# One core, three layers in a hand-written order: all 1277 steps re-ordered, and one drain of GpSimd

## The chip, the cores and the metric

One NeuronCore of a Trainium2 chip. The metric is device microseconds of one execution; the kernel before was run three times: 381.22, 381.32 and 378.41 us, median 381.22.

## The reference

Three layers one behind the other, in float32 (cut to the core):

```python
# 1. WKV attention: r, k, v are (2, 8, 768, 48)
for t in range(S):
    cur = einsum('bhd,bhe->bhde', u * k[:, :, t], v[:, :, t])
    y[:, :, t] = einsum('bhd,bhde->bhe', r[:, :, t], state + cur)
    state = w * state + einsum('bhd,bhe->bhde', k[:, :, t], v[:, :, t])
# 2. gated FFN: x is (2, 768, 384), d_ff 1024
h = maximum(x @ w_in, 0)
conv = depthwise_conv3(h, conv_w)          # along the sequence
x = (h * sigmoid(conv)) @ w_out
# 3. one expert of 8 per token; the expert before is kept while the local gate is 0.5 or more
logits = x @ w_gate;  local = sigmoid(x @ w_local)
e = argmax(logits[b, s]) if s == 0 or local[b, s] < 0.5 else prev_e
out[b, s] = softmax(logits[b, s])[e] * (maximum(x[b, s] @ w1[e], 0) @ w2[e])
```

## The kernel before, in words

Products are formed from float16 halves: each float32 operand is split into a high part (ScalarE) and the low rest (VectorE or GpSimd), and PE makes three passes: high by high, high by low, low by high.

The attention runs in 12 chunks of 128 tokens and both batches of heads: decay (A), bonus (B), state (Z) and scores (Y), fed by loads (L) and tables (T, C). The FFN works on blocks of 256 hidden rows (G) and output tiles (O, and apart as OL for the logits and OR for the rows). WI and WO load and split its weights. Routing (R, Q, S) finds expert, slot and probability of each token and scatters the rows to a table of slots in DRAM on GpSimd; FE and F count the tokens per expert and make the lists of rows. F's last DVE line is L867.

The experts work on 14 tiles: 0 to 3 are full tiles of early tokens, 4 to 9 are pairs of half tiles with two experts each, 10 to 13 full tiles of later tokens. A tile's tokens are fetched by I: GpSimd gathers rows from slots into yb (L977), SP transposes them in the DMA into xsT (L993). ER loads the early rows er by two DMAs of SP, and EX multiplies them into place (L952, L954, xe). Each tile goes twice through U and D, once for each half of d_ff. U is nine products per half tile (L1049, ph), the split of the relu (ACT L1029 and DVE L1031, hr) and a transposition of hr into hT: eight PE transposes (L1061, the copy is L1064), or for the pairs a DMA transpose on SP (L1056). D multiplies hT with W2 (L1073, py); in the first half ACT scales (L1080), in the second DVE adds (L1082) and GpSimd scatters the rows to the output (L871). The weights W1 and W2 come by SP (L961, L967), 768 KB each into one of three staging buffers, and are split by ACT (L497) and DVE (L154).

Each of these works is a generator, and the order of everything is one written list, SEQ: every token advances the generator of its name by one step (up to its next yield). The engines PE, ACT, DVE and SP issue in exactly the order in which SEQ emits their instructions; GpSimd's instructions are chained in that order too (pool_order), except DMAs among themselves. So a step that is moved carries all its instructions, on every engine, with it. At the end a branch (L1126, on the number of tiles that 14 didn't cover, with the value loaded at L1125) holds a fallback that isn't taken with these inputs; L1168 is the end of the program.

Of the splits of hr:

```python
def relu_split(hi, lo, ps):
    nc.scalar.activation(out=hi, in_=ps, func=AF.Relu)
    yield
    nc.vector.scalar_tensor_tensor(out=lo, in0=ps, scalar=0.0, in1=hi, op0=ALU.max, op1=ALU.subtract)
```

Of the kernel before, what the change touches and what calls it, by code (L numbers as in the profile page):

```python
# [54 lines left out]
G_0_0_1 A_3 A_3 WI_2 WO_0 Y_2 B_3 B_3 B_3 Y_3 Y_3 L_5 L_5 L_5 L_5 Z_3 G_0_0_1 WI_2 Y_3 G_0_0_1 G_0_0_1 A_5 A_4 A_4 A_4 Y_2 Y_2 WO_1 Z_4 B_3 WO_0 WO_0
WI_2 Y_2 L_6 L_6 G_0_0_1 Y_4 WO_2 G_0_0_1 G_0_0_1 WO_0 WO_0 A_5 A_5 A_5 B_4 B_4 WO_0 WO_0 G_0_0_1 G_0_0_2 G_0_0_2 Y_3 Y_3 L_6 L_6 A_6 G_0_0_2 WO_1
G_0_0_2 WO_1 G_0_0_2 G_0_0_2 A_6 L_9 B_4 Y_4 G_0_0_1 A_5 A_6 Y_4 G_0_0_0 WO_1 G_0_0_0 G_0_0_2 G_0_0_0 B_5 Y_3 G_0_0_2 G_0_0_2 Z_6 WO_2 A_6 A_6 A_5 A_5
Y_4 WO_1 WO_1 G_0_0_0 Y_3 Y_3 L_7 L_7 Y_3 WO_1 Y_5 B_4 L_7 L_7 A_7 WO_1 WO_1 B_5 A_7 A_6 Y_4 Z_6 G_0_0_2 G_0_0_0 A_6 A_6 G_0_1_1 G_0_0_0 WO_2 A_7 B_5
# [24 lines left out]
G_1_2_2 OR_1_0 G_1_2_2 G_1_2_2 R_1_2_2 OR_1_1 W1_7_0 R_1_2_2 R_1_2_2 G_1_2_2 G_1_2_2 G_1_2_2 R_1_2_2 R_1_2_2 Q_1_2_2 OR_1_2 Q_1_2_2 OR_1_2 S_2 S_2
G_1_2_0 Q_1_0_2 Q_1_0_2 S_7 S_7 G_1_2_0 S_5 S_5 W1_7_0 G_1_2_2 OR_1_2 OR_1_2 G_1_2_3 FE G_1_2_2 OR_1_0 OR_1_0 G_1_2_3 G_1_2_0 S_3 S_3 OR_1_2 OR_1_2
G_1_2_2 W1_2_0 G_1_2_2 G_1_2_2 G_1_2_2 FE OR_1_0 OR_1_0 OR_1_0 W1_0_0 S_6 S_6 OL_1_5 OL_1_5 OR_1_3 OR_1_3 OL_1_4 OL_1_4 OR_1_3 OL_1_5 OR_1_3 OR_1_3
Q_1_2_2 OL_1_4 W1_1_0 W1_0_0 OL_1_4 FE W1_1_0 OR_1_3 OL_1_4 OL_1_4 OL_1_5 OL_1_5 OL_1_5 OR_1_5 R_1_4_2 OR_1_5 W1_1_0 VE VE R_1_4_2 R_1_4_2 OR_1_4
OR_1_4 W1_4_0 W1_4_0 R_1_4_2 R_1_4_2 R_1_4_2 S_8 S_8 S_9 S_9 OR_1_5 OR_1_5 R_1_4_2 R_1_4_2 W1_4_0 R_1_4_2 IO BL_0 Q_1_4_2 F OR_1_5 OR_1_5 OR_1_4
Q_1_4_2 Q_1_4_2 W2_2_0 ER ER I_1 I_0 OR_1_4 I_2 I_3 S_11 S_11 OH OH OR_1_4 OR_1_4 S_10 S_10 W1_2_0 W1_2_0 I_1 I_0 I_2 I_3 W2_1_0 EX EX EX EX F EX EX
EX EX U_0_1 EX EX EX EX U_0_0 U_0_2 U_0_3 W2_3_0 F M M U_0_1 U_0_1 BL_1 BL_2 I_6 I_7 U_0_4 W2_2_0 U_0_0 U_0_0 U_0_5 U_0_1 EJ W2_2_0 U_0_2 U_0_2 U_0_1
U_0_0 I_8 I_9 I_10 I_11 I_12 I_13 U_0_3 U_0_3 W2_1_0 U_0_0 U_0_4 U_0_4 U_0_2 W2_1_0 U_0_4 U_0_2 W2_6_0 I_6 U_0_5 U_0_5 V V U_0_3 U_0_5 I_7 U_0_6 U_0_3  # L90
W2_3_0 I_8 U_0_7 U_0_6 U_0_6 W2_3_0 U_0_6 I_9 W2_4_0 U_0_8 U_0_7 U_0_7 W2_6_0 U_0_7 I_10 U_0_9 W2_6_0 U_0_8 U_0_8 U_0_8 I_11 I_12 W2_7_0 U_0_10 W2_4_0
U_0_9 U_0_9 W2_4_0 U_0_9 W2_5_0 I_13 U_0_11 U_0_10 U_0_10 U_0_10 U_0_10 W2_7_0 U_0_12 U_0_11 U_0_11 W2_7_0 U_0_11 W2_0_0 U_0_11 U_0_13 W2_5_0 ME ME ME
U_0_12 U_0_12 W2_5_0 U_0_12 U_0_13 U_0_13 U_0_12 W2_0_0 U_0_13 W2_0_0 U_0_13 D_0_4 W1_5_1 D_0_5 D_0_4 W1_4_1 D_0_3 D_0_3 W1_4_1 D_0_2 D_0_2 W1_5_1
D_0_5 D_0_10 D_0_10 W1_3_1 W1_3_1 D_0_1 W1_4_1 W1_5_1 D_0_12 D_0_6 D_0_6 W1_6_1 W1_7_1 W1_3_1 W1_6_1 W1_6_1 D_0_13 W1_7_1 W1_7_1 U_1_4 D_0_13 W1_0_1
# [1078 lines left out]
```

## Time and profile before

| | us |
|---|---|
| median of three runs | 381.22 |
| the profiled execution | 378.47 |
| its span | 376.6 |
| PE busy | 322.8 (86%) |
| DVE busy | 260.8 (69%) |
| ACT busy | 192.1 (51%) |
| GpSimd (POOL) busy | 186.3 (49%) |
| mean granted TensorE clock | 0.941 |

All times in the views are microseconds from the start of the span of the profiled execution. A row of a timeline has start, duration, engine, line, operation and tiles, and in brackets how long the engine was idle before it and what released it. In a table of windows the busy time and the number of instructions of PE, PEld, DVE, ACT and POOL, in this order, stand behind the length of the stretch, then the mean granted clock of TensorE (1.00 is the higher of its two levels, 0.50 the lower), the DMA engines' share and GB/s.

### The profile page before, as it was taken

Reading aid. Unit: us, or ns where it says so; the run is one execution under the profiler, and the core shown is the slowest. Engines: PE = TensorE matmul, PEld = TensorE weight load, DVE = VectorE, ACT = ScalarE, POOL = GpSimd, SP = SyncE. Lnnn points to the kernel's source line nnn. Section 1 sums busy time; section 2 is a strip of 40 time slices with the busy share of each in tenths; the row PEclk is TensorE's granted clock in tenths of the full one; section 3 lists DMA queues with packets and bytes.
Section 4 is the critical chain, followed back from the end, with each engine's and each line's share of the span. In section 5 each row is a group of like instructions: output and inputs, shape, how many; then the busy total and the mean of one; then the engine's idle time right before and its main releaser. Section 6 shows DMA issues by size and latency. Waiting matters only on the chain. (4 is left out here: it accounts for less than half of the span.)

```text
span 376.6 us, 7931 instructions
## 1 busy us (share of the span) xinstructions
PE 322.8 (86%) x2859; PEld 223.1 (59%) x2859; DVE 260.8 (69%) x497; ACT 192.1 (51%) x343; POOL 186.3 (49%) x222
## 2 busy tenths in 40 slices
...
GB/s 203 224 187 222 161 166 123 102 127 77 128 150 89 84 138 23 158 243 179 46 162 191 240 240 44 222 60 229 266 204 174 225 258 256 278 39 57 126 95 52
DMA packets 106880, 58.81 MB, mean 156 GB/s; under 512 B 87171, under 2 KB 96599, under 8 KB 106836
## 3 DMA queue, kind: packets, MB, share of 16 engines
...
q14 instruction: 18, 0.15, 0.2%
HBM read 41.57 MB, written 5.96 MB: 126 GB/s over the span
## 5 line engine op out<-in xcount | busy, mean ns | idle before, releaser
L871 POOL DMA_INDIRECT out_dram<-yb x14 | 13.8, 987 | 117.1 <-DVE yb L1082 114.4
L1049 PE MATMUL ph<-w1h,xsT 128*128 (+1 forms) x144 | 49.7, 412 | 15.1 <-DMA xsT<-yb 15.1
L1073 PE MATMUL py<-w2h,hT 128*64 (+2 forms) x320 | 56.9, 327 | 0.0
L599 PE MATMUL psh<-x1T,wi_h 128*128 128x258 f16 (+2 forms) x288 | 49.5, 273 | 1.4 <-ACT hp L604 1.4
L1049 PEld LDWEIGHTS <-xsT 128*128 128x128 f16 (+1 forms) x216 | 22.7, 109 | 42.4 <-DMA xsT<-yb 16.0
L1073 PEld LDWEIGHTS <-hT 128*64 128x64 f16 (+1 forms) x480 | 34.4, 105 | 21.3 <-issue 2.8
L1031 DVE SCALAR_TENSOR_TENSOR hr<-ph,hr 128x512 f16<-128x512 f32 x28 | 18.9, 685 | 33.1 <-ACT hr L1029 30.0
L599 PE MATMUL psh<-x1T,wi_l 128*128 128x258 f16 (+2 forms) x144 | 39.3, 273 | 0.0
L154 DVE SCALAR_TENSOR_TENSOR w1l<-ws,w1h 128x1536 f16<-128x1536 f32 x16 | 27.9, 1755 | 14.8 <-ACT w1h L497 14.7
L1073 PE MATMUL py<-w2l,hT 128*64 128x384 f16 (+2 forms) x160 | 37.2, 326 | 0.0
L646 PE MATMUL psx<-wo_h,g_l 128*128 128x384 f16 (+2 forms) x144 | 35.9, 278 | 1.2 <-POOL g_l L152 1.2
L646 PE MATMUL psx<-wo_l,g_h 128*128 128x384 f16 (+2 forms) x144 | 36.6, 278 | 0.0
L152 POOL TENSOR_TENSOR g_l<-cv,g_h 128x512 f16<-128x512 f32 (+2 forms) x31 | 31.7, 1034 | 9.5 <-ACT g_h L163 9.4
L646 PE MATMUL psx<-wo_h,g_h 128*128 128x384 f16 (+2 forms) x144 | 36.3, 279 | 0.0
L154 DVE SCALAR_TENSOR_TENSOR w2l<-ws,w2h 128x1536 f16<-128x1536 f32 x16 | 28.0, 1753 | 7.1 <-ACT w2h L497 7.0
L599 PEld LDWEIGHTS <-wi_h 128*128 128x128 f16 x288 | 27.3, 98 | 7.2 <-issue 1.8
L1029 ACT ACTIVATE hr<-ph 128x512 f16<-128x512 f32 x28 | 16.7, 600 | 28.6 <-PE ph L1049 25.3
L646 PEld LDWEIGHTS <-g_h 128*128 128x128 f16 x288 | 22.5, 98 | 11.9 <-issue 1.1
L1049 PE MATMUL ph<-w1l,xsT 128*128 (+1 forms) x72 | 29.5, 409 | 0.0
L604 ACT ACTIVATE hp<-psh 128x258 f32<-128x258 f32 (+2 forms) x47 | 17.9, 383 | 21.1 <-PE psh L599 19.1
L497 ACT ACTIVATE w2h<-ws 128x1536 f16<-128x1536 f32 x16 | 23.7, 1488 | 9.1 <-DMA ws<-in_moe_w_dram 8.2
L1064 ACT COPY hT<-pt 128x1024 f16<-128x1024 f16 x16 | 16.1, 1016 | 19.7 <-PE pt L1061 19.7
...
## 6 DMA issues: line engine op xcount, KB each, us to landing
...
```

Of the source, the lines that this page charges most:

```text
L152: eng.tensor_tensor(out=lo, in0=src, in1=hi, op=ALU.subtract)
L154: nc.vector.scalar_tensor_tensor(out=lo, in0=src, scalar=scale, in1=hi, op0=ALU.mult, op1=ALU.subtract)
L497: nc.scalar.activation(out=hi, in_=src, func=AF.Copy, scale=scale)
L599: nc.tensor.matmul(ps[:, 0:n], lhsT=x[:, kk, ft * P:(ft + 1) * P], rhs=x1T[b][:, y, t0:t0 + n], start=(i == 0), stop=(i == 3 * NK - 1))
L604: nc.scalar.activation(out=hp[:, a, o:o + n], in_=ps[:, 0:n], func=AF.Relu, scale=2.0 ** -8)
L646: nc.tensor.matmul(ps[:, c0:c1], lhsT=x[part][:, ft, o:o + P], rhs=y[:, ft, c0:c1], start=(n == 0), stop=(n == 3 * NF - 1))
L871: q = nc.gpsimd.indirect_dma_start(out=dst, out_offset=bass.IndirectOffsetOnAxis(ap=idx.bitcast(U32), axis=0), in_=src, in_offset=None, bo ...
L1029: nc.scalar.activation(out=hi, in_=ps, func=AF.Relu)
L1031: nc.vector.scalar_tensor_tensor(out=lo, in0=ps, scalar=0.0, in1=hi, op0=ALU.max, op1=ALU.subtract)
L1049: nc.tensor.matmul(ps[hs], lhsT=xs_, rhs=part(W[("w1h", "w1l")[y]], o + kk * HF, HF), start=(n == 0), stop=(n == 3 * NK - 1))
L1064: nc.scalar.copy(out=W["hT"][i], in_=pt)
L1073: nc.tensor.matmul(ps[hs], lhsT=hT[:, x * KF + ft, hs], rhs=part(W[("w2h", "w2l")[y]], o + ft * DM, DM), start=(n == 0), stop=(n == 3 * KF ...
```

## The change

The list SEQ is written anew: the same tokens, each as often as before, in another order, and one token DR more. Trailing tokens of a generator that has nothing left stand at random places and do nothing. DR is a new step that issues one drain on GpSimd; it stands behind the last gathers of the late tiles and ahead of the first output scatter. The four hr buffers were four tiles of a list (popped when a tile's split begins, appended when it has been transposed); they are now taken in turn from a pool's tag with four buffers. The configuration is unchanged. Behind the two insertions lines move by 4 or 5: L1031 is L1036, L1056 is L1061, L1073 is L1076, L1125 is L1129, L1126 is L1130 and L1168 is L1172.

```diff
 SEQ = """
-C C LD C WI_0 C C WO_0 C C C CV C H_1 H_1 C C H_0 H_0 LD LD T T WI_3 LD C LD C WI_0 ...
...
+C C C LD C C WI_0 CV T LD C T T T T WO_0 LD L_2 WI_0 WI_0 C LD WI_0 CV C C LD T LD ...
...
-        W["hr"] = [late.tile([P, 2 * HF], F16, name=f"hr{i}") for i in range(4)]
+        late.tile([P, 2 * HF], F16, name="hr", tag="hr", bufs=4)
...
+    def drain():
+        nc.gpsimd.drain()
+        yield
...
-        hr = W["hr"].pop(0)
+        hr = W["late"].tile([P, 2 * HF], F16, name="hr", tag="hr", bufs=4)
         yield from relu_split(hr[:, 0:HF], hr[:, HF:2 * HF], ps)
...
-            W["hr"].append(hr)
...
-        W["hr"].append(hr)
...
+        "DR": drain,
```

Three places of the new order, engine by engine. First SP, behind the load of the expert numbers (ej) and ahead of the late tiles: ws is a staging buffer for expert weights, xsT6 and so on are late tiles' transposed tokens, hT4 and so on transposed hidden rows. Before:

```order
L1125 TENSOR_LOAD ej_140
L1125 ISA x2
L1056 DMA_TRANSPOSE hT4_3342<-hr0_3334 128x8x128
L967 DMA ws_3478<-in_moe2_w2_dram 128x4x384
L993 DMA_TRANSPOSE xsT6_3354<-yb1_3332 128x6x64
L1056 DMA_TRANSPOSE hT5_3343<-hr1_3335 128x8x128
L993 DMA_TRANSPOSE xsT7_3355<-yb1_3332 128x6x64
L993 DMA_TRANSPOSE xsT8_3356<-yb1_3332 128x6x64
L1056 DMA_TRANSPOSE hT6_3344<-hr2_3336 128x8x128
L993 DMA_TRANSPOSE xsT9_3357<-yb1_3332 128x6x64
L967 DMA ws_3558<-in_moe2_w2_dram 128x4x384
```

And now:

```order
L1129 TENSOR_LOAD ej_140
L1129 ISA x2
L967 DMA ws_3409<-in_moe2_w2_dram 128x4x384
L993 DMA_TRANSPOSE xsT6_3332<-yb1_3313 128x6x64
L993 DMA_TRANSPOSE xsT11_3337<-yb2_3314 128x6x128
L993 DMA_TRANSPOSE xsT10_3336<-yb2_3314 128x6x128
L993 DMA_TRANSPOSE xsT7_3333<-yb1_3313 128x6x64
L993 DMA_TRANSPOSE xsT12_3338<-yb2_3314 128x6x128
L967 DMA ws_3510<-in_moe2_w2_dram 128x4x384
L993 DMA_TRANSPOSE xsT8_3334<-yb1_3313 128x6x64
L1061 DMA_TRANSPOSE hT5_3321<-hr_3477 128x8x128
```

The hT transposes, which stood between the xsT ones, now stand behind six of them, and the first one is that of tile 5 and not 4.

Next DVE, in the last routing group: from the end of FE (rows1) to the one-hot oc, which PE needs (L736, pso). lg are the logits, xr the routed rows, w1l the low part of expert weights. Before:

```order
L812 TENSOR_TENSOR rows1_143<-em1_2919,jp_129 128x4
L154 SCALAR_TENSOR_TENSOR xr_125<-psx_2953,xr_125 128x384
L651 TENSOR_SCALAR lg_126<-psx_2966 128x9
L651 TENSOR_SCALAR lg_126<-psx_2940 128x9
L714 TENSOR_REDUCE mxs_136<-lg_126 128x2
L716 TENSOR_TENSOR oh_3045<-lg_126,mxs_136 128x16
L718 TENSOR_TENSOR oh_3045<-oh_3045,iom_127 128x16
L720 TENSOR_REDUCE mn_3048<-oh_3045 128x2
L721 TENSOR_TENSOR oh_3045<-iom_127,mn_3048 128x16
L723 TENSOR_SCALAR fr_3051<-lg_126 128x2
L727 TENSOR_TENSOR oc_3053<-oh_3045,fr_3051 128x2x8
L728 TENSOR_SCALAR oc_3053<-fr_3051 128x2x8
L154 SCALAR_TENSOR_TENSOR w1l_2279<-ws_3010,w1h_2278 128x1536
```

And now:

```order
L812 TENSOR_TENSOR rows1_143<-em1_3005,jp_129 128x4
L714 TENSOR_REDUCE mxs_136<-lg_126 128x2
L716 TENSOR_TENSOR oh_3073<-lg_126,mxs_136 128x16
L718 TENSOR_TENSOR oh_3073<-oh_3073,iom_127 128x16
L720 TENSOR_REDUCE mn_3076<-oh_3073 128x2
L721 TENSOR_TENSOR oh_3073<-iom_127,mn_3076 128x16
L723 TENSOR_SCALAR fr_3079<-lg_126 128x2
L727 TENSOR_TENSOR oc_3081<-oh_3073,fr_3079 128x2x8
L728 TENSOR_SCALAR oc_3081<-fr_3079 128x2x8
L154 SCALAR_TENSOR_TENSOR w1l_2300<-ws_2898,w1h_2299 128x1536
L742 SCALAR_TENSOR_TENSOR seq_133<-ca_3093,seq_133,pso_3088 8x256
L154 SCALAR_TENSOR_TENSOR w1l_2300<-ws_2760,w1h_2299 128x1536
```

The split of xr and the two logits, which stood between rows1 and mxs, are gone from there (they stand earlier), and the scan follows after one w1l as before.

Last GpSimd, at the end of the program; yb1 and yb2 hold the results of the tiles, out_0_dram is the output. Before:

```order
L986 MEMSET yb2_3333 128x4
L977 DMA yb2_3333<-slots_139,rows_146 128x392
L871 DMA out_0_dram<-yb2_3333 1536x384
L1126 UNCONDITIONAL_BRANCH
L1126 ISA
L1126 UNCONDITIONAL_BRANCH
L1168 ISA
```

And now:

```order
L977 DMA yb2_3314<-slots_139,rows_146 128x392
L871 DMA out_0_dram<-yb2_3314 1536x384
L1130 UNCONDITIONAL_BRANCH
L1130 ISA
L1130 UNCONDITIONAL_BRANCH
L871 DMA out_0_dram<-yb1_3313 1536x384
L1172 UNCONDITIONAL_BRANCH
L1172 ISA
```

Of the 14 output scatters one has moved behind the branch; before, all 14 stand ahead of it (the scatters of yb2 shown first in both belong to the fallback). GpSimd's gathers of late tiles are in the order 6, 11, 10, 13, 7, 12, 8, 9, where they were in the order 6 to 13, and the iota and the first blanking stand some routing groups earlier. On PE the matmul of F's count (L819), which stood ahead of the products of EX, is behind the first of six; D_0_5, D_0_4 and the transposes of the last tiles are set between the late U, where all late U stood ahead of D_0_4. On SP the two loads of er, which stood behind a W2 load, stand behind the load W1_2_0 and ahead of that W2 load. On DVE the tables RQ and G and narrowings of the weights WI_0 and WO_0 stand ahead of rT and kT at the start.

## Rows read from the trace of the kernel before

**Rows 1.** The windows of the stages (busy us, instructions, clock, DMA).
```profile
40.00:200.00 160.00, 151.85 (x1553) 120.61 (x1551) 138.62 (x297) 95.37 (x212) 121.78 (x153) 1.00 0.59 127
200.00:220.00 20.00, 13.61 (x89) 7.51 (x90) 14.10 (x41) 6.08 (x9) 9.63 (x10) 0.91 0.92 197
220.00:240.00 20.00, 12.65 (x102) 7.18 (x99) 12.40 (x34) 11.62 (x14) 13.15 (x14) 0.91 0.51 147
240.00:260.00 20.00, 11.45 (x77) 6.58 (x78) 6.99 (x7) 5.11 (x6) 0.00 (x0) 0.76 0.71 174
260.00:280.00 20.00, 16.52 (x109) 8.16 (x108) 8.53 (x8) 10.73 (x12) 0.00 (x0) 0.82 0.92 230
280.00:365.00 85.00, 84.59 (x684) 48.00 (x678) 43.10 (x41) 43.89 (x51) 10.88 (x11) 1.00 0.57 171
```

**Rows 2.** The waits of PE: us in all, times, longest.
```profile
PE ph L1049 <- DMA xsT<-yb: 15.1, 4, 8.7
```

**Rows 3.** PE's timeline from 202 to 277 us, at its gaps.
```profile
202.49 0.59 PE L736 MATMUL pso<-id,oc 128*8 128x128 f16 x4 [4.93 <-DVE oc L728]
...
214.66 0.38 PE L952 MATMUL pse<-idk,er 128*128 128x128 f16 x4 [3.90 <-DMA er<-slots]
...
243.75 0.58 PE L1049 MATMUL ph<-w1h,xsT 128*64 x1 [8.73 <-DMA xsT<-yb]
...
258.18 0.59 PE L1049 MATMUL ph<-w1h,xsT 128*128 x1 [3.31 <-DMA xsT<-yb]
...
271.10 0.59 PE L1049 MATMUL ph<-w1h,xsT 128*128 x1 [1.55 <-DMA xsT<-yb]
...
276.40 0.35 PE L1073 MATMUL py<-w2h,hT 128*64 128x384 f16 x2
```

**Rows 4.** SP's timeline from 204 to 260 us.
```profile
204.01 1.27 SPq L929 DMA_DIRECT2D er<-slots  x2
...
236.31 1.25 SPq L1056 DMA_TRANSPOSE hT<-hr  x1
...
238.37 1.21 SPq L993 DMA_TRANSPOSE xsT<-yb  x1
...
257.25 2.65 SPq L993 DMA_TRANSPOSE xsT<-yb  x2
```

**Rows 5.** GpSimd's timeline from 199 to 228 us.
```profile
199.63 0.62 POOL L938 IOTA places<- 128x512 f32 x1
200.17 1.40 POOL L985 MEMSET yb<- 128x1536 int32 x1
...
226.44 0.99 POOL L977 DMA_INDIRECT yb<-slots,rows  x1 [2.78 <-issue]
```

**Rows 6.** The timelines of DVE and PE at the start.
```profile
12.20 0.69 DVE L148 TENSOR_TENSOR rT<-ptf,Q 128x512 f32<-128x512 f32 x1 [0.25 <-PE ptf L325]
...
41.11 0.38 PE L599 MATMUL psh<-x1T,wi_h 128*128 128x256 f16 x2
```

**Rows 7.** DVE in routing: line L723 (ns min/median/max, first and last start), timeline.
```profile
L723 DVE TENSOR_SCALAR fr<-lg x4: 160/162/2145, 139.8 to 199.5; 128x2 f32<-128x2 f32 x3, 128x6 f32<-128x6 f32 x1
...
201.82 1.75 DVE L154 SCALAR_TENSOR_TENSOR w1l<-ws,w1h 128x1536 f16<-128x1536 f32 x1
...
212.70 1.76 DVE L154 SCALAR_TENSOR_TENSOR w1l<-ws,w1h 128x1536 f16<-128x1536 f32 x1 [0.66 <-ACT w1h L497]
...
225.81 0.15 DVE L867 TENSOR_TENSOR ej<-cc 1x1 int32<-1x1 f32 x1
```

**Rows 8.** The end: timeline, and GpSimd's queue in lines L1126 and L1168.
```profile
365.31 1.67 DVE L1082 SCALAR_TENSOR_TENSOR yb<-py,yb 128x384 f32<-128x384 f32 x3 [6.06 <-PE py L1073]
...
368.78 0.98 POOL L871 DMA_INDIRECT out_dram<-yb  x1 [0.30 <-POOLq L1126]
...
L1126 POOLq INC_SWDGE_SEM  x1: 940/940/940, 371.6 to 371.6; - x1
...
L1168 POOLq DRAIN  x3: 40/107/3177, 372.6 to 376.3; - x3
```

More of the change, by code (lines that the diff above doesn't have):

```diff
@@ L55 @@
[L55 to L58, printed above, removed]
@@ L83 @@
[L83 to L86, printed above, removed]
@@ L87 @@
[L87 to L94, printed above, removed]
@@ L99 @@
-U_1_9 U_1_3 W2_1_1 D_1_5 D_1_6 D_1_6 D_1_13 U_1_12 D_1_13 U_1_8 U_1_8 U_1_8 U_1_3 D_1_1 D_1_6 D_1_1 D_1_0 D_1_0 D_1_0 D_1_1 U_1_2 D_1_2 U_1_3 U_1_9
-D_1_12 U_1_3 D_1_12 D_1_3 D_1_8 D_1_5 U_1_9 U_1_7 D_1_8 U_1_10 U_1_7 U_1_10 D_1_13 U_1_10 D_1_9 D_1_3 D_1_3 D_1_8 D_1_12 D_1_9 D_1_9 U_1_10 U_1_10
-D_1_11 D_1_10 D_1_2 D_1_2 D_1_7 D_1_10 D_1_10 D_1_11 D_1_11 D_1_7 D_1_7
+C C C LD C C WI_0 CV T LD C T T T T WO_0 LD L_2 WI_0 WI_0 C LD WI_0 CV C C LD T LD C WI_3 C H_2 L_2 H_1 LD LD WO_0 A_0 T L_2 T A_1 A_0 A_0 C A_0 A_0
@@ new lines @@
+G_0_0_2 Y_3 G_0_0_2 Y_3 G_0_0_1 L_6 G_0_0_2 G_0_0_0 Y_4 WO_1 L_5 L_6 G_0_0_1 WO_0 A_5 B_4 G_0_0_0 Z_3 G_0_0_2 L_7 A_5 Y_3 A_6 A_5 Y_2 G_0_0_2 Y_2 A_5
+A_6 G_0_0_0 WO_1 A_6 A_6 Y_4 WO_1 Y_3 G_0_0_2 WO_0 WO_1 Y_4 Z_4 G_0_0_1 A_5 G_0_0_2 B_4 Y_4 WO_0 A_5 Y_3 L_7 G_0_0_0 G_0_0_2 Z_4 A_5 G_0_0_0 WO_1
+G_0_0_2 L_7 WO_2 L_7 G_0_0_2 Y_5 A_6 WO_1 WO_1 G_0_0_0 G_0_0_0 B_5 Z_6 Y_3 A_7 Y_4 WO_2 B_5 Y_3 H_1 G_0_0_0 Y_5 G_0_0_0 G_0_0_2 WO_1 G_0_1_1 G_0_1_2
+G_0_1_1 G_0_1_2 WO_1 G_0_1_1 Z_6 A_7 A_6 Y_5 A_6 L_8 WO_1 G_0_1_2 Y_4 WO_2 G_0_1_1 G_0_1_2 A_7 G_0_1_1 G_0_1_1 G_0_1_1 G_0_0_0 WO_0 G_0_1_1 A_6
@@ new lines @@
+B_7 WO_3 Y_7 WO_3 G_0_1_3 Y_7 A_8 G_0_1_3 B_7 G_0_0_3 Y_6 A_8 O_0_2 Y_7 A_8 G_0_2_0 G_0_0_3 O_0_2 G_0_1_3 WO_3 WO_3 RC G_0_2_0 O_0_2 Y_6 L_11 G_0_2_0
+G_0_2_0 A_8 L_9 B_7 G_0_2_0 WO_2 G_0_2_1 Z_8 Y_7 G_0_2_0 Y_6 Z_7 G_0_1_3 L_9 G_0_2_0 B_8 Y_7 WO_3 A_9 WO_3 G_0_2_1 A_9 A_8 G_0_2_0 A_8 B_7 WO_3 A_8
+G_0_2_1 A_9 G_0_2_0 Y_8 O_0_1 Y_7 L_10 L_11 O_0_1 B_8 A_9 G_0_2_1 G_0_2_1 A_9 O_0_1 G_0_2_1 G_0_2_1 G_0_2_0 G_0_2_1 G_0_2_2 Z_7 L_10 Z_8 G_0_2_2
+G_0_2_0 G_0_2_1 Y_7 L_10 O_0_2 Y_8 O_0_2 O_0_0 G_0_2_0 O_0_0 Y_8 G_0_2_1 O_0_1 A_9 L_10 Y_7 O_0_1 G_0_2_3 Z_8 A_9 G_0_2_2 A_9 B_8 Y_8 B_9 O_0_0 H_2
@@ new lines @@
+A_10 A_9 B_8 G_0_2_1 Y_8 O_0_0 G_0_2_3 W1_6_0 G_0_2_2 Z_9 O_0_3 O_0_2 O_0_1 G_0_2_1 Y_9 G_0_2_2 G_0_2_2 Y_8 B_9 Y_9 Y_9 G_0_2_2 A_10 Y_7 Z_9 Y_8 O_0_2
+Y_6 G_0_2_2 G_0_2_3 A_10 G_0_2_2 G_0_2_2 O_0_3 A_10 Y_9 A_10 G_0_2_3 Y_8 G_0_2_2 Z_10 Y_8 G_0_2_3 G_0_2_3 G_0_2_3 G_0_2_2 O_0_1 RC O_0_4 O_0_4 L_11
+G_1_0_3 G_1_0_3 O_0_4 G_0_2_3 G_1_0_3 G_0_2_3 G_1_0_3 Z_8 SI G_1_0_3 G_1_0_3 A_10 Y_9 O_0_3 G_1_0_3 L_11 A_10 G_0_2_3 G_0_2_3 A_11 G_1_0_1 A_10
+G_0_2_3 O_0_3 A_10 Z_9 G_1_0_1 G_1_0_3 B_9 WO_3 B_10 Y_10 O_0_5 O_0_4 O_0_3 O_0_3 O_0_3 Y_10 A_11 B_10 H_0 W1_5_0 G_1_0_1 O_0_5 G_1_0_3 G_1_0_3
@@ new lines @@
+R_0_0_6 G_1_1_1 G_1_1_1 G_1_1_1 OL_1_1 G_1_1_1 G_1_1_2 R_0_0_6 G_1_0_2 G_1_1_1 G_1_1_1 G_1_0_2 G_1_1_3 BL_0 R_0_0_6 G_1_1_2 OL_1_1 G_1_1_2 G_1_1_1
+OL_1_1 G_1_1_2 R_0_0_6 G_1_1_2 G_1_1_2 G_1_1_1 OL_1_1 OL_1_1 G_1_1_3 Q_0_0_6 G_1_1_3 G_1_1_3 G_1_1_3 R_0_0_6 OL_1_0 OR_1_1 G_1_1_3 G_1_1_2 OR_1_1
+G_1_1_3 G_1_1_3 OL_1_0 OL_1_0 OL_1_0 G_1_1_1 G_1_1_0 W1_6_0 G_1_1_1 R_0_0_6 S_3 G_1_1_2 OL_1_0 G_1_1_3 OR_1_1 G_1_1_2 G_1_1_3 OL_1_1 G_1_1_2 G_1_1_0
+R_1_0_2 W1_5_0 G_1_2_1 G_1_2_1 G_1_1_0 G_1_1_2 W1_6_0 G_1_2_1 W1_3_0 G_1_1_0 G_1_2_1 G_1_2_1 X W1_5_0 G_1_1_0 G_1_1_2 S_4 G_1_2_1 W1_7_0 G_1_2_1
@@ new lines @@
+OR_1_2 Q_1_2_2 G_1_2_0 IO W1_0_0 G_1_2_2 R_1_2_2 OR_1_3 OR_1_2 G_1_2_0 OR_1_2 OR_1_2 W1_1_0 Q_1_2_2 OR_1_0 S_0 R_1_2_2 R_1_2_2 OR_1_3 G_1_2_2 W1_1_0
+G_1_2_2 R_1_2_2 R_1_2_2 FE Q_1_2_2 OR_1_0 G_1_2_2 S_4 OR_1_0 S_7 OR_1_3 G_1_2_2 OR_1_3 R_1_2_2 OL_1_4 S_2 W1_4_0 S_8 OR_1_0 OL_1_4 OL_1_5 OL_1_5
+OL_1_5 FE OR_1_3 OL_1_5 S_6 OR_1_3 S_9 OL_1_4 OL_1_3 OL_1_4 OL_1_5 OR_1_4 W1_2_0 OR_1_4 ER OL_1_4 OR_1_4 FE R_1_4_2 I_2 ER R_1_4_2 R_1_4_2 W1_1_0
+W1_2_0 R_1_4_2 S_8 W1_4_0 S_1 OR_1_5 OR_1_5 W2_2_0 R_1_4_2 R_1_4_2 OR_1_4 OR_1_4 OR_1_5 OR_1_4 R_1_4_2 I_2 R_1_4_2 Q_1_4_2 VE OR_1_5 R_1_4_2 OH I_3
@@ new lines @@
+Q_1_4_2 OR_1_5 W1_2_0 OH I_1 EX EX F I_1 EX Q_1_4_2 EX F OR_1_5 I_0 EX S_10 EX EX S_11 I_3 EX EX VE F EX EJ I_0 EX EX W2_6_0 U_0_2 U_0_0 M W2_2_0
+U_0_1 S_0 ME W2_2_0 BL_1 U_0_0 U_0_2 U_0_1 U_0_0 W2_3_0 V U_0_4 U_0_2 I_6 BL_2 W2_1_0 I_11 U_0_1 U_0_1 I_10 W2_1_0 I_13 S_7 U_0_0 V U_0_5 I_6 W2_1_0
+U_0_2 I_7 I_12 W2_6_0 U_0_5 I_8 U_0_3 U_0_4 I_11 I_10 U_0_0 I_7 U_0_5 U_0_11 S_5 I_12 W2_4_0 U_0_4 U_0_10 W2_6_0 U_0_11 U_0_11 U_0_3 I_8 U_0_11 U_0_3
+U_0_7 WO_1 U_0_3 U_0_5 W2_7_0 U_0_10 W2_3_0 I_13 W2_4_0 W2_4_0 U_0_6 M S_3 U_0_3 W2_5_0 U_0_11 U_0_7 W2_7_0 U_0_1 U_0_10 U_0_7 U_0_12 I_9 U_0_4 S_11
```

58 lines of the change are left out of this document (26 added, 32 removed).

## The prediction

> **What bounds the kernel now.** I read the windows first, then PE's waits, PE's gaps, and only then the other engines beside each gap. The windows [rows 1] show two stages that PE fills and one that it does not. From 40 to 200 us PE is busy 151.85 of 160 us, and from 280 to 365 us 84.59 of 85, both at full granted clock. Between 200 and 280 us it is busy 13.61 + 12.65 + 11.45 + 16.52 = 54.23 of 80 us, and the granted clock there is 0.91, 0.91, 0.76 and 0.82: part of even that busy time runs at the lower of the two levels. So 25.8 us of waiting lie in one stage, the turn from routing to the experts, and an order that only moves steps can win there and hardly anywhere else. The list of PE's waits [rows 2] names the largest reason: 15.1 us in four waits for xsT, the transposed tokens of the late tiles. The gaps [rows 3] place them: 4.93 us before 202.49 (routing's one-hot on DVE), 3.90 before 214.66 (the early rows er), 8.73 before 243.75, 3.31 before 258.18 and 1.55 before 271.10 (xsT, with a small fourth). PE is past the first half's U at 276.40, where D_0_4 starts.
>
> The SP rows [rows 4] say why xsT is late. The gathers on GpSimd begin at 226.44 [rows 5]. The first late transpose leaves SP only at 238.37, because the hT transpose of U_0_4 stands ahead of it and waits until 236.31 for its hr. The later ones are laced with five more hT transposes and with weight loads, so that SP issues xsT as late as 257.25. PE used the first 243.75 - 238.37 = 5.4 us after its issue.
>
> **The change part by part.** The sum is made against the profiled execution: 378.47 us, span 376.6 and 1.9 around it. The shown runs have their median at 381.22, 2.75 above it; one of the three (378.41) is as fast.
>
> Start. The tables RQ and G and two narrowings of weights move ahead of rT on DVE, which stands at 12.20 [rows 6]; rT then comes some 5 us later. The weight chain behind it ends at about the same place in DVE's order, and the first gate matmul, now at 41.11, needs both. Bounds: 5 us lost (nothing made up) to 3 won (rT's chain is not last, the weights are). I take -0.5, near the cover, since the same DVE work stands ahead of that matmul.
>
> Attention and gate stage. 151.85 of 160 us are PE work that the change neither adds to nor removes. At most 8.15 us can be won. On the other side nothing but DVE's own slack holds: DVE is busy 138.62 of 160. I take -1, range -4 to +8.
>
> Routing. DVE's chain to the one-hot stands at lg and mxs behind a copy of xr, and its L723 takes 2.15 us [rows 7], beside IOTA and MEMSET on GpSimd from 199.63 to 201.57 [rows 5]. The line's other instructions take 0.16. The new order puts the chain directly behind rows1, and IOTA and blanking far earlier. If both come true, R, the moment at which the one-hot is done (201.82), comes 0.6 + 2.0 us earlier; bounds 0 and 2.6; I take 1.8, so R = 200.0.
>
> The Trainium skill, page "SBUF — State Buffer", section "Who interferes with whom", says that DVE and GpSimd share one pair of ports and that whoever issues second is blocked for the other's whole instruction. By it the 2 us go wherever the two overlap, and may come back where the new order sets DVE's small steps beside another GpSimd memory operation; the row agrees with the blocking, no row shows the new places. By the rule alone R would gain 2.0 and not 1.8.
>
> Early rows. The two loads of er now stand behind the third weight load W1_2_0, whose buffer is freed by a split that DVE does two splits later: one split (the one at 201.82) is 1.75 us [rows 7], and two with the small steps between end at R + 3.9. Before, er was issued at 204.01 [rows 4] = R + 2.2, and PE could go on at 214.66 = R + 12.8. Issued at R + 4.6, the same transfer ends at R + 15.2. This is 2.4 us given back, and PE waits here about 9 us instead of 3.9. The count F#1, whose matmul stood ahead of EX, stands behind EX's first step now, so the numbering on DVE starts at R + 16.3. Before it was itself held by a split (212.70 to 214.45 [rows 7]) and ended at 225.96 = R + 24.1; that split stands behind it now, and it ends at R + 25.1 by the same 8 us of steps. The gathers follow 0.5 us later: R + 25.5 = 225.5, against 226.44: -0.9.
>
> Late tiles. No hT transpose stands ahead of the first six late xsT on SP now; each waits for its own gather alone. A GpSimd DMA is counted as landed 2.8 us after its start (368.78 to 371.6 [rows 8]); the transpose and its landing take the 5.4 us seen above, and the first late tile is the second in order, 1.3 us on. So the first full wait ends 2.8 + 1.3 + 5.4 = 9.5 us, with two hand-overs between queues some 10.1 us, after the first gather, where it took 243.75 - 226.44 = 17.3: -7.2. From the first late U to the last (U_0_13) went 271.10 - 243.75 = 27.4 us. In the new order the last one's transpose stands behind a W2 load that waits for a split behind U_0_7; counting splits of 1.75 and tiles of nine matmuls, it starts at R + 55.5 = 255.5, 20 us after the first (R + 35.6): -7.4. Behind the last one stood 276.40 + 4.0 (D_0_4 and D_0_5) - 271.10 = 9.3 us; now D_0_5, waiting for its weights until about R + 59, D_0_4, the transposes and U_0_9 end at R + 67.7, 12.2 us on: +2.9. Together -0.9 - 7.2 - 7.4 + 2.9 = -12.6. Against it stands the clock. After 8.73 us idle the windows show it at 0.76; the wait before EX is now of that length, and EX and the first U behind it, some 6 us, may run at the lower level. +2.6, range 0 to 5. I take -10 for the stage; range -16 (two thirds of the idle gone) to 0 (the time only changes its place).
>
> Second half. 84.59 us of PE work without a gap. The weights of the second half start loading about as far ahead of the first U_1 as before, but reach it with a reserve of some 5 us. What the earlier end takes away of this cover costs +1.5, range 0 to 5.
>
> The end. Three L1082 follow the last matmul at 365.31, the last scatter starts at 368.78, GpSimd counts its transfers until 372.5 and then drains for 3177 ns [rows 8]. Two things change. The added drain stands where GpSimd idles for 90 us, so that it costs nothing itself; if the last drain's time goes with the DMAs since the one before, 14 instead of 38 leave 1.2 of 3.2 us. And the last scatter now stands behind the branch, so it waits for the landing of all others and for the 0.94 us that follow. One of these two gives up to 2 and the other costs about 0.8: -1.2, range -3 to +2.
>
> Sum: -0.5 - 1 - 10 + 1.5 - 1.2 = -11.2, 378.47 - 11.2 = 367.3. Two of three runs lie above the profiled one, so I forecast 368.
>
> **The rivals.** (a) The slack only changes place. The wait before EX grows (9 against 3.9), F#1 stands behind it, and the gathers start 2 or 3 us later than before instead of 0.9 earlier, if R gains nothing and er lands late; the idle clock eats the rest. For it: the longest chain through here is not PE's but DVE's and the DMAs'. Against it: the hT transposes did stand ahead of xsT in SP's rows. Then the stage gives 5 instead of 10, the reserve of W1 is gone, and start and middle give nothing: 378.47 - 5 + 3 = 376.5, between 373 and 381.
> (b) Slower. In the stage from 40 to 200 us DVE is 87% busy and in strict order. A new order of all its steps that meets the waits of PE, ACT and GpSimd less well makes DVE the bound there. At 78%, 138.62 / 0.78 = 178 us stand in place of 160: 18 us more, less 10 in the turn: 378.47 + 18 - 10 = 386. It decides from about 14 us of lost overlap on. For it: rT 5 us late at the start of every chain. Against it: PE's 0 to 1.4 us idle per window says that a good interlacing exists, and the steps of one chain keep their order.
> (c) More than I count: all xsT waits go, the clock stays up, and the start and the end win too: 378.47 - 15.1 - 3 = 360.
>
> **How the numbers follow.** Forecast (363 to 373) 0.50, (c) 0.11, (a) 0.23, (b) 0.16. This kernel's measurements can tell about 1% from no change, so faster is below 377.4 and slower above 385.0. Forecast, (c) and a third of (a) are faster: 0.69. The rest of (a) is within 1%: 0.15. (b) is slower: 0.16. The range leaves out the half of (b) beyond 386 and the far end of (c): 358 to 386.
>
> **What would show it.** Right: PE's gaps before xsT are one of about 9 us before EX and two or three below 4 us; L723 takes 0.2; SP issues the first six late xsT without an hT between; D_0 starts near 262 to 268; the last scatter stands alone behind the others' landing, and the last drain is near 1.2 us. Wrong: PE's idle time between 40 and 200 us above 12 us (then (b)); the first late U not before 241 (then (a)); a drain of 3 us at the end again (then the added drain does nothing).

## The result, and the profile after

| | before | after |
|---|---|---|
| median | 380.29 us (4 runs, 378.41 to 381.32) | 358.48 us (4 runs, 356.92 to 359.28) |
| ratio, 95% interval | | 0.9427 (0.9373 to 0.9481) |
| the profiled execution, its span | 378.47, 376.6 | 358.66, 356.8 |
| PE busy | 322.8 | 318.0 |
| mean granted TensorE clock | 0.941 | 0.965 |

The kernel takes 5.7% less time. Medians, here and below, are of all runs; ratios, which are what is compared, are the recorded ones and leave out a few executions at a lower clock, so they are not the quotients of two medians. The forecast was 368 us in a range of 358 to 386: the direction was right, the gain of some 20 us in the profile is nearly twice the 11.2 that were summed. The windows of after in the stretches of [rows 1], with the same columns:

```profile
0.00:20.00 20.00, 7.64 (x36) 4.44 (x36) 14.86 (x37) 5.68 (x9) 8.69 (x18) 0.94 0.88 212
20.00:40.00 20.00, 17.89 (x148) 15.22 (x150) 17.32 (x23) 8.30 (x18) 15.41 (x12) 0.63 0.72 179
40.00:200.00 160.00, 155.65 (x1622) 123.78 (x1617) 137.53 (x290) 101.58 (x227) 124.38 (x158) 1.00 0.59 132
200.00:220.00 20.00, 14.53 (x101) 8.19 (x101) 17.00 (x68) 6.34 (x10) 9.94 (x8) 1.00 0.87 198
220.00:240.00 20.00, 15.84 (x102) 7.28 (x100) 10.65 (x23) 6.74 (x9) 10.53 (x14) 0.91 0.81 207
240.00:260.00 20.00, 20.00 (x178) 11.65 (x178) 11.38 (x11) 15.82 (x17) 0.00 (x0) 1.00 1.10 250
260.00:280.00 20.00, 19.73 (x155) 11.24 (x153) 11.64 (x10) 14.68 (x19) 0.00 (x0) 1.00 0.88 244
```

From 200 to 280 us PE idled 25.8 us; now 9.9, all but 0.3 of it in the first half of the stretch. The clock fell to 0.76 there and now stays at 1.00 but for 0.91 in one window. In the first 20 us PE does less than before (7.64 us against 13.18). Its longest waits (us in all, times, longest):

```profile
PE psT L304 <- DVE G L299: 7.6, 1, 7.6
PE ph L1054 <- issue: 4.2, 1, 4.2
PE psa L442 <- DVE kT L148: 3.5, 1, 3.5
PE ptf L340 <- POOL full L148: 3.4, 2, 2.2
PE pse L954 <- DVE xr L154: 2.1, 1, 2.1
```

Three of the five (G, kT, full) stand in the start. The second, 4.2 us, stands before the first late U; "issue" means that the profile names nothing that it waited for. It is the rest of the wait for xsT: two other profiles name xsT as the releaser of this gap, 2.50 us in a second one of after (after_again below) and 4.40 in after without its drain (no_drain below):

```profile
236.87 0.58 PE L1054 MATMUL ph<-w1h,xsT 128*128 x1 [4.40 <-DMA xsT<-yb]
```

So of 15.1 us of waiting for xsT 2.5 to 4.4 are left. PE's timeline at the points of [rows 3], and in the start up to the first gate matmul ([rows 6] has it for before):

```profile
20.82 2.08 PE L442 MATMUL psa<-rT,kT 64*128 64x128 f32 x16 [3.46 <-DVE kT L148]
...
45.38 0.38 PE L599 MATMUL psh<-x1T,wi_h 128*128 128x256 f16 x2
...
204.50 0.39 PE L736 MATMUL pso<-id,oc 128*8 128x128 f16 x4 [1.42 <-DVE oc L728]
...
210.91 0.39 PE L952 MATMUL pse<-idk,er 128*128 128x128 f16 x4
...
217.28 0.39 PE L954 MATMUL pse<-hot,xr 128*128 128x512 f16 x1 [2.06 <-DVE xr L154]
...
236.58 0.59 PE L1054 MATMUL ph<-w1h,xsT 128*128 x1 [4.16 <-issue]
...
251.68 0.39 PE L1054 MATMUL ph<-w1h,xsT 128*128 x1
253.72 0.35 PE L1076 MATMUL py<-w2h,hT 128*64 128x384 f16 x2
...
260.43 0.34 PE L1076 MATMUL py<-w2h,hT 128*128 x1
```

One gap of 4.16 us stands before the first late U at 236.58; from there over U_0_13 at 251.68, D_0_5 at 253.72 and D_0_4 to the end of the last U, U_0_9, at 260.43 there is no gap of half a microsecond. Before, the first half was done 20 us later: D_0_4 and D_0_5 began at 276.40 [rows 3] and took 4.0.

The other engines there, SP first (as [rows 4]), then GpSimd (as [rows 5]), then DVE (as [rows 6, 7], with line L723):

```profile
202.49 1.27 SPq L929 DMA_DIRECT2D er<-slots  x2
...
229.22 8.43 SPq L993 DMA_TRANSPOSE xsT<-yb  x5
...
238.38 2.19 SPq L993 DMA_TRANSPOSE xsT<-yb  x1
240.62 1.30 SPq L1061 DMA_TRANSPOSE hT<-hr  x1
```

```profile
189.44 0.63 POOL L938 IOTA places<- 128x512 f32 x1
...
223.93 1.15 POOL L977 DMA_INDIRECT yb<-slots,rows  x1 [3.36 <-DMA slots<-xr,posi]
...
226.85 1.05 POOL L977 DMA_INDIRECT yb<-slots,rows  x1 [0.27 <-POOL yb L987]
```

```profile
19.06 0.68 DVE L148 TENSOR_TENSOR rT<-ptf,Q 128x512 f32<-128x512 f32 x1
...
L723 DVE TENSOR_SCALAR fr<-lg x4: 159/160/165, 145.3 to 204.0; 128x2 f32<-128x2 f32 x3, 128x6 f32<-128x6 f32 x1
...
201.53 0.29 DVE L651 TENSOR_SCALAR lg<-psx 128x9 f32<-128x9 f32 x2 [2.62 <-remote]
...
204.34 1.75 DVE L154 SCALAR_TENSOR_TENSOR w1l<-ws,w1h 128x1536 f16<-128x1536 f32 x1
...
221.45 0.15 DVE L867 TENSOR_TENSOR ej<-cc 1x1 int32<-1x1 f32 x1
```

SP's first late transpose leaves at 229.22 and not at 238.37, and six xsT pass before the first hT. L723 is back at 0.16 us. rT is 7 us later. The one-hot (done where the w1l split begins) comes at 204.34, 2.5 later than before. The numbering ends 17.3 us behind it, where it took 24.1.

The end (as [rows 8]; the row of the drain added, L1014, stands last):

```profile
347.88 0.33 PE L1076 MATMUL py<-w2h,hT 128*64 x2
...
348.67 0.62 DVE L1085 SCALAR_TENSOR_TENSOR yb<-py,yb 128x384 f32<-128x384 f32 x1 [1.88 <-PE py L1076]
...
352.70 0.97 POOL L871 DMA_INDIRECT out_dram<-yb  x1 [4.04 <-DMA out_dram<-yb]
...
L1172 POOLq DRAIN  x3: 46/112/3382, 352.5 to 356.5; - x3
...
L1014 POOLq DRAIN  x1: 11572/11572/11572, 229.7 to 229.7; - x1
```

One scatter stands alone behind the landing of the others, as the order said. The last matmul of before, for comparison, is this row; the end behind it took 376.6 - 364.59 = 12.0 us and now takes 356.8 - 348.21 = 8.6:

```profile
364.26 0.33 PE L1073 MATMUL py<-w2h,hT 128*64 x2
```

With these rows the 19.8 us fall into five stretches (measured: of after less of before; predicted: the terms of the sum that lie in it):

| stretch | before | after | measured | predicted |
|---|---|---|---|---|
| start to first gate matmul | 41.11 | 45.38 | +4.3 | -0.5 |
| to the one-hot | 160.7 | 159.0 | -1.8 | -2.8 |
| to the first late U | 41.9 | 32.2 | -9.7 | -6.3 |
| to the last matmul | 120.8 | 111.6 | -9.2 | -0.4 |
| to the end of the span | 12.0 | 8.6 | -3.4 | -1.2 |

### The profile page after: what moved, and what is told of

The parts are those of the page before. It is cut to its first block, busy times and chain, and to the rows that moved or that the text cites. A ratio compares the mean times of both kernels' runs of the same rounds, so it can differ in the third digit from the quotient of the medians.

```text
span 356.8 us, 7923 instructions
## 1 busy us (share of the span) xinstructions
PE 318.0 (89%) x2859; PEld 218.4 (61%) x2859; DVE 256.1 (72%) x497; ACT 191.6 (54%) x343; POOL 182.7 (51%) x222
## 4 chain that ended last, share of the span: by engine, by line
PE 35%; issue 32%; DVE 12%; DMA 8%; POOL 6%; ACT 4%; POOLq 1%; another core or an unknown queue 1%; SPq 0%; DVEq 0%; ACTq 0%
PE psx L646 9%; PE psh L599 8%; PE psy L451 5%; PE psa L442 3%; DMA out_dram<-yb 3%; PE pst L613 2%; POOL out_dram L871 2%; POOL yb L977 2%; DMA raw<-in_moe_w_in_dram 2%; PE ptf L340 2%; DMA slots<-xr,posi 2%; PE psy L462 2%; DVE w1l L154 1%; DVE ps L621 1%; DMA lT<-full 1%
## 5 line engine op out<-in xcount | busy, mean ns | idle before, releaser
L1076 PE MATMUL py<-w2h,hT 128*128 (+2 forms) x320 | 57.9, 328 | 0.8 <-issue 0.8
L1054 PE MATMUL ph<-w1h,xsT 128*128 (+1 forms) x144 | 47.0, 389 | 4.4 <-issue 4.2
L1076 PEld LDWEIGHTS <-hT 128*64 128x64 f16 (+1 forms) x480 | 34.3, 105 | 23.9 <-issue 5.8
L1054 PEld LDWEIGHTS <-xsT 128*128 128x128 f16 (+1 forms) x216 | 21.2, 103 | 29.9 <-issue 10.3
L152 POOL TENSOR_TENSOR g_l<-cv,g_h 128x512 f16<-128x512 f32 (+2 forms) x31 | 32.6, 1060 | 12.4 <-ACT g_h L163 11.2
L1076 PE MATMUL py<-w2l,hT 128*128 (+2 forms) x160 | 37.2, 326 | 0.3 <-DVE w2l L154 0.3
L646 PE MATMUL psx<-wo_h,g_h 128*128 128x9 f16 (+2 forms) x144 | 35.8, 275 | 0.8 <-issue 0.8
L646 PE MATMUL psx<-wo_l,g_h 128*128 128x9 f16 (+2 forms) x144 | 35.8, 274 | 0.4 <-issue 0.4
L646 PE MATMUL psx<-wo_h,g_l 128*128 128x9 f16 (+2 forms) x144 | 35.6, 274 | 0.0
L1054 PE MATMUL ph<-w1l,xsT 128*128 (+1 forms) x72 | 27.8, 386 | 0.4 <-DVE w1l L154 0.4
L497 ACT ACTIVATE w1h<-ws 128x1536 f16<-128x1536 f32 x16 | 23.6, 1479 | 2.8 <-DMA ws<-in_moe_w_dram 2.4
```

What stands on the lines that cost most here:

```text
L152: eng.tensor_tensor(out=lo, in0=src, in1=hi, op=ALU.subtract)
L497: nc.scalar.activation(out=hi, in_=src, func=AF.Copy, scale=scale)
L646: nc.tensor.matmul(ps[:, c0:c1], lhsT=x[part][:, ft, o:o + P], rhs=y[:, ft, c0:c1], start=(n == 0), stop=(n == 3 * NF - 1))
L1054: nc.tensor.matmul(ps[hs], lhsT=xs_, rhs=part(W[("w1h", "w1l")[y]], o + kk * HF, HF), start=(n == 0), stop=(n == 3 * NK - 1))
L1076: nc.tensor.matmul(ps[hs], lhsT=hT[:, x * KF + ft, hs], rhs=part(W[("w2h", "w2l")[y]], o + ft * DM, DM), start=(n == 0), stop=(n == 3 * KF ...
```

## The experiments

Two kinds. Small edits take the order of before and move a few steps. Hybrids take the order of one kernel up to a cut, and then whatever is left in the order of the other; at a cut 13 to 21 steps stand on different sides of it in the two orders, so a hybrid also has a seam that neither order has. All of them have the code of after, with its hr buffers; b_rt, which has little else that is new, takes 0.9978 of before, so the buffers by themselves are worth nothing that shows. Each set has its own runs of before on its chip, so the ratios are what is compared.

**SP's order alone (b_sp).** On the order of before:

```diff
 W2_1_0
-U_0_4
 U_0_2 W2_6_0 I_6
+I_7 I_8 I_9 I_10 I_11 U_0_4
 U_0_5 U_0_5 V V U_0_3 U_0_5
-I_7
 U_0_6 U_0_3 W2_3_0
-I_8
...
```

> The order of before; only the SP transposes of late tiles 6 to 11 are moved ahead of the hT transpose of U_0_4, PE, DVE and ACT as before. Theory (SP's order keeps the late tiles back): first late U near 237 instead of 243.75, D_0_4 near 262 to 268 instead of 276.4, time 366 to 371 where before has 379 to 381. Rival (the gain needs D_0_4 and D_0_5 set between the late U on PE, or the earlier numbering): the xsT waits move to the later tiles, D_0_4 not before 272, time 375 to 380.

372.57 us, 0.981 (0.9715 to 0.9906): a gain, but one between what the theory and what the rival expected. The first late U starts at 238.99, 4.8 us earlier than before, but D_0_4 only at 272, as the rival had it. PE's waits say where it went, and then SP and ACT:

```profile
PE pt L1065 <- ACT hr L1034: 5.2, 1, 5.2
PE pt L1065 <- DVE hr L1036: 3.9, 3, 1.9
PE pse L952 <- DMA er<-slots: 3.3, 1, 3.3
PE ph L1054 <- DMA xsT<-yb: 2.4, 2, 1.5
```

```profile
232.38 12.61 SPq L993 DMA_TRANSPOSE xsT<-yb  x6
245.08 4.03 SPq L1061 DMA_TRANSPOSE hT<-hr  x3
249.16 0.58 SPq L967 DMA_DIRECT2D ws<-in_moe_w_dram  x1
```

```profile
256.13 1.48 ACT L497 ACTIVATE w2h<-ws 128x1536 f16<-128x1536 f32 x1 [7.06 <-DMA ws<-in_moe_w_dram]
```

The wait for xsT fell from 15.1 to 2.4 us. But the W2 loads now stand on SP behind six xsT and three hT. ACT, in order, waits 7.06 us for one of them until 256.13 with the relus of later tiles queued behind it, and PE waits for these. Here the queue that was freed for one kind of transfer made another late.

**The numbering alone (b_rt).** On the order of before:

```diff
 S_10 S_10
+F
 W1_2_0 W1_2_0 I_1 I_0 I_2 I_3 W2_1_0 EX EX EX EX
-F
 EX EX
+F
 EX EX U_0_1 EX EX EX EX U_0_0 U_0_2 U_0_3 W2_3_0
-F
 M M
```

> The order of before; only two steps of the numbering F are moved on DVE and POOL: F's second step ahead of the last W1 split, its third ahead of the copies of the later EX steps. Theory: F's last line ends 3 to 5 us earlier and the late gathers start 2 to 3 us earlier, but SP's first late transpose still stands behind the hT transpose of U_0_4 that waits until 236: time within 1% of before, 377 to 381. Rival (the numbering is what is last): 373 to 376.

378.24 us, 0.9978 (0.9936 to 1.002). The numbering ended at 223.94 with the one-hot at 203.5: 20.4 us behind it and not 24.1. The gathers began at 226.81, and PE's wait stayed:

```profile
246.43 0.58 PE L1054 MATMUL ph<-w1h,xsT 128*64 x1 [8.23 <-DMA xsT<-yb]
```

The 3.7 us won on DVE are worth nothing here, for two reasons. SP holds the transposes back, as the theory had it. And the gathers gained less than it expected: they began 23.4 us behind the one-hot, where it took 24.6 before, because they then stood behind GpSimd's blanking of yb (L987):

```profile
226.81 0.99 POOL L977 DMA_INDIRECT yb<-slots,rows  x1 [0.16 <-POOL yb L987]
```

**Both (b_sp_rt).**

> Both of the two small edits on the order of before. Theory: they add, since with SP's order mended the gathers are last: first late U near 234, time 363 to 368, 2 to 4 us below the SP edit alone. Rival (the two don't add): as the SP edit alone.

368.0 us, 0.9682 (0.9607 to 0.9758): 1.3% below the SP edit alone, where the numbering alone gave nothing. The two intervals overlap, but every one of the four runs is faster than every one with the SP edit alone. With SP mended the earlier numbering does pay. The first late U:

```profile
236.58 0.38 PE L1054 MATMUL ph<-w1h,xsT 128*64 x1 [1.12 <-DMA xsT<-yb]
```

That is 35.3 us behind the one-hot (201.27), where before took 41.9 and after takes 32.2. From there to the end of the last matmul (356.19) it takes 119.6 us, as in before (120.8), where after takes 111.6. So these two edits make 6.6 of the 9.7 us of the third stretch of the table, and hardly anything of the fourth.

**Cut at the start of the D steps (x_half).**

```diff
-SEQ = before
+SEQ = before up to step 1100, then the rest in the order of after
```

> The order of before up to the start of the first half's D steps (1100 steps), then the rest in the order of after, with the drain. Theory (the second half of after loses some 3.4 us of PE's time and its end wins some 3.2): the two cancel, 376 to 380, within 1% of before; last matmul 3 us later, 3 us fewer behind it. Rival (after's second half is better in itself): 372 to 375.

381.1 us, 0.9994 (0.9958 to 1.003). After's second half and end behind before's first half are worth nothing in sum. What either is worth by itself this run doesn't tell.

**Cut behind the numbering (x_u).**

```diff
-SEQ = before
+SEQ = before up to step 988, then the rest in the order of after
```

> The order of before up to the end of the numbering F (988 steps), then the rest in the order of after, with the drain. Theory (the late phase, U with SP's transposes and D_0_4, D_0_5 between, makes 8 to 13 us of the gain, the routing in front of it 8 or more): 365 to 370. Rival (the late phase is all of it): as the cut one stage earlier, 353 to 357.

364.43 us, 0.9611 (0.9532 to 0.969), a little below the expected range. The steps between this cut and the one before (the late U with SP's transposes, D_0_4, D_0_5 and the W2 splits) are worth 0.9994 - 0.9611 = 3.8%, some 15 us. One xsT wait of 4.95 us before 240.14 is left, since numbering and gathers are those of before. From that first late U to the end of the last matmul (351.45) it takes 111.3 us, as in after (111.6): the fourth stretch of the table comes with the order behind the numbering.

**Cut at the last routing group (x_turn, x_turn_again).**

```diff
-SEQ = before
+SEQ = before up to step 912, then the rest in the order of after
```

> The order of before up to the last routing group (its first 912 steps), then everything that is left in the order of after, with the drain. Theory (the gain lies behind that point, and after only loses 2.6 us ahead of it by its slower start): 354 to 357, below after. Rival (the turn of after is fast because of what after's DVE and SP did ahead of that point): 358 to 366.

353.23 us, 0.9281 (0.9191 to 0.937). It looked as if it beat after, so it was measured again beside after on one chip:

> The changed kernel itself, on the chip of the three runs with it. Theory: 0.94 of before, as in the first measurement; the hybrid x_turn lies 1 to 2% below it.

> The kernel of x_turn once more, beside after on one chip. Theory (after loses 4 us by its start and 2 to 3 in the last routing steps ahead of the one-hot, and nothing behind makes it up): 0.925 to 0.93 of before, 4 to 6 us below after, one-hot done 5 to 7 us earlier than in after. Rival (the difference between the two was that of two chips): the same time as after within 1%.

After: 357.89 us, 0.9414 (0.9374 to 0.9453). The hybrid: 357.45 us, 0.9392 (0.9346 to 0.9438). The theory's 4 to 6 us are not there; the rival, one time within 1%, fits. The ten runs of the hybrid lie between 351.69 and 361.31. In its first profile, on the first chip, the one-hot is done at 197.66 and the last matmul at 342.90, 6.7 and 5.3 us ahead of after; the runs beside after show none of that, so it can't be counted. Against x_u, which ran on another chip, the routing steps are worth 2.2% to 3.3%, some 8 to 13 us.

**Cut at the first gate step (x_front).**

```diff
-SEQ = before
+SEQ = before up to step 151, then the rest in the order of after
```

> The order of before up to the first gate step (151 steps), then the rest in the order of after, with the drain. Theory (after's start loses 4.3 us by the late rT and kT, and nothing behind makes it up): 353 to 356, first gate matmul near 41.1. Rival (the start's loss is hidden by what waits later): 358 to 360 as after.

357.63 us, 0.9416 (0.9344 to 0.9489): the same ratio as after. In its trace the first gate matmul starts at 42.16 and not 45.38, the first late U at 232.10 and the last matmul ends at 346.10. On the same chip the run without the drain (next) has 45.02, 236.87 and 349.15 there. So in the profiles 3 us of the start reach the end; in the ratios against after none does. What the slow start costs, between nothing and 3 us, stays open.

**After without its drain (no_drain).**

```diff
-W2_3_1 U_1_13 DR U_1_12 U_1_9
+W2_3_1 U_1_13 U_1_12 U_1_9
```

> After without its drain of GpSimd. Theory (the drain lies in GpSimd's idle time and doesn't shorten the last one): the same time, 357 to 360, last drain of GpSimd 3.2 to 3.4 us. Rival (the last drain's length goes with the DMAs since the drain before): the last drain grows by 2 us or more, 360 to 362.

361.24 us, 0.9465 (0.9378 to 0.9552), which by itself can't be told from after. GpSimd's last drain can:

```profile
L1172 POOLq DRAIN  x3: 40/113/4382, 353.9 to 358.8; - x3
```

4.38 us where after has 3.38, and where the six other runs with after's end and the early drain have 3.37 to 3.39: the theory (no effect) fell, the rival's mechanism holds with 1.0 us and not 2.

**Before's second half behind after's turn (x_best, x_best_ed).**

```diff
-SEQ = before up to step 912, then the rest in the order of after
+SEQ = that up to the last U of the first half, then the rest in the order of before
...
+DR_1
```

The last line is that of x_best_ed alone.

> As x_turn up to the last U of the first half, then what is left in the order of before; one drain of GpSimd behind the gathers as in after. Theory (before's second half is free of gaps and 3.4 us shorter, before's end 2.3 longer): 1 us below x_turn, within 1%; last matmul 3 us earlier. Rival (before's second half was free of gaps only because the weights had time while PE waited): gaps before U_1 and D_1, no gain or a loss.

363.66 us, 0.9493 (0.9424 to 0.9561), 1% above x_turn_again: no gain, as the rival had it, but not for its reason. The gaps stand at the cut, before the last transposes and the remaining D of the first half:

```profile
261.48 0.40 PE L1065 MATMUL pt<-idk,hr 128*128 128x128 f16 x4 [2.63 <-ACT hr L1034]
...
263.76 0.48 PE L1076 MATMUL py<-w2h,hT 128*128 x1 [1.16 <-ACT w2h L497]
...
265.55 0.48 PE L1076 MATMUL py<-w2l,hT 128*128 x1 [1.32 <-DVE w2l L154]
```

They are 5.4 us in all. Behind them, from 266 us to the last matmul, PE is busy without a gap (85.47 of 85.47 us), so the weights of before's second half are not late here; the rival would have them late. The first gap is not the weights' either: ACT's relu of the last full tile waited until 260.82 for an hr buffer that a hT transpose still had to read (four of these stand one behind the other on SP from 254.86), and the W2 splits stand behind that relu. The run with one more drain, below, has the same gaps. So what was lost was lost at the seam of the two orders, and whether before's second half would pay behind after's turn stays open. In this kernel all 14 scatters stand ahead of the branch, behind one drain as in after, and the last drain is this:

```profile
L1172 POOLq DRAIN  x3: 46/107/1202, 359.1 to 360.8; - x3
```

1.20 us, where before had 3.18 without the early drain [rows 8].

> As x_best, with one more drain of GpSimd right behind the last of the 14 output scatters, ahead of the branch. Theory (the last drain works off something that builds up with GpSimd's DMAs and can run while the last scatter's landing is waited for): the last drain falls from 3.2 to 3.4 us to under 1, the end comes 1 to 3 us earlier than in x_best. Rival (the last drain's length is its own, or the added one delays the count of the landings by as much): no gain.

362.31 us, 0.9545 (0.9506 to 0.9585): no gain. The last drain falls to 0.11 us, but the added one takes 4.73 from 352.6 on, while the last two scatters run, and holds GpSimd, which then counts the landings:

```profile
L1172 POOLq DRAIN  x3: 46/58/107, 358.8 to 360.0; - x3
...
L1014 POOLq DRAIN  x2: 4726/8176/11627, 225.7 to 352.6; - x2
```

No version was found that surely beats after.

## Why the prediction was right, and where its sum was off

What bounded the kernel was read rightly: the waits lay in the turn, xsT was the largest, and SP's hT transposes stood ahead of it. b_sp shows it by taking that wait away (15.1 to 2.4 us) with nothing else new but the hr buffers, though about half of the 12.7 us came back as other waits. The direction followed from that. The size was right by luck: 358.48 lies half a microsecond inside the range and outside the 363 to 373 that the forecast itself was given, and the errors of the five stretches (+4.8, +1.0, -3.4, -8.8 and -2.2 us) partly cancel.

Start: taken as -0.5 with 5 us lost as its bound; measured +4.3 in the trace. The weights were not the last there: PE waits 3.46 us for kT (at 20.82), and runs at a clock of 0.63 from 20 to 40 us, where before had 0.71. The cover that the prediction named was not one.

Middle and the one-hot: -2.8 against -1.8. The routing term came true: from the last step of FE (rows1) to the one-hot DVE takes 1.2 us instead of 3.9, 2.7 won where 1.8 was taken and 2.6 was the bound. L723 took 0.16 and not 2.15, as expected, with IOTA gone to 189.44. The prediction weighed the Trainium skill's page "SBUF — State Buffer" (section "Who interferes with whom"), by which the one of DVE and GpSimd that issues second is blocked; the page says so of DVE instructions in a two-port mode and of some with two inputs, a condition that the prediction leaves out, and no run here shows the mode of L723. The rows agree in that the operation is short without IOTA and MEMSET; beside the issue of a gather (203.43 to 204.47) it was not held up. What was lost, 1.0 us where 1 was to be won, stands ahead of rows1: DVE idles 2.62 us before it takes the logits at 201.53. The row names no engine as releaser, and PE's last products for the logits end at 199.5, so what DVE waited for stays open. R itself came at 204.34 and not at 200.0; 4.3 us of this are the start's.

To the first late U: -6.3 against -9.7. First gather to first late U took 12.7 us, not 10.1: a blanking of yb stands between the first gather and the second, which came 2.9 us later and not 1.3. The larger error, the other way, was ahead of that: er was issued at 202.49, before the one-hot, and not at R + 4.6. The prediction took the third W1 load to wait for a split behind the one-hot; its buffer came free earlier. So the wait of 9 us before EX never came (its own rows, 3.9 us and 2.4 more, give 6.3), the first step of EX started at 210.91, and the numbering was done at R + 17.3 and not R + 25.1. Before, its last step stood on DVE behind the copy of the last EX product (the one that b_rt moves).

To the last matmul: -0.4 against -9.2, the term that was mis-sized most. From the first late U to the end of the first half the prediction counted 32.2 us and 2.6 more for the clock, with waits for a W2 load before U_0_13 and for the weights of D_0_5. It took 260.43 - 236.58 = 23.9, with no such wait, where before took 36.65. In that stretch PE idled 8.3 us before and not at all now, and it is busy 28.4 us before and 23.9 now with the same 188 matmul instructions, at a mean granted clock of 0.82 and of 0.94. So the clock, taken as a loss, gave back some 4.3 us: before, PE ran at half rate behind three of its four waits for xsT (its products 0.43 us apart instead of 0.215), and now only for some 3 us behind the one gap of 4.16. The part that was foreseen was too small: the second half takes 348.21 - 260.43 = 87.8 us against 84.2, +3.6 and not +1.5; 1.75 of it is idle time, the rest longer busy time, with the transposes of U_0_13, which now stand there. b_sp_rt shows that this stretch is not the doing of SP's order and the numbering alone (119.6 us), and x_u that it comes with the order behind the numbering (111.3 us). What in that order makes it, the D steps between the late U, the order of the tiles or the earlier places of the W2 splits, wasn't taken apart.

The end: -1.2 against -3.4. That the last drain goes with GpSimd's DMAs since the one before is borne out, 1.20 us in x_best as the prediction had it. In after it reads 3.38, because the scatter behind the branch starts with it. The prediction named a drain of 3 us at the end as the sign that the added one does nothing; that sign misled, since without the added one it is 4.38. The rest is the order of the last tiles: before, three L1082 ran together behind the last matmul and three scatters queued 1.28 us apart; after, one L1085 is left.

Of the other signs named ahead, L723, the six xsT without an hT between and the lone scatter came; the 9 us before EX did not, and D_0 started at 253.72, well ahead of 262. Of the rivals, (c) (more than counted, 360, chance 0.11) came nearest, though not by its start. (b) named the stage from 40 to 200 us, and PE idles less there than before (4.35 against 8.15 us). (a) failed because the wait before EX shrank.
